# Making the last six of thirty x * v units of the second batch beside the first batch's third step

## The chip, the cores and the metric

The kernel runs on one core of one Trainium2 chip. Its engines are TensorE (PE in the profile; PEld is its weight load), VectorE (DVE), ScalarE (ACT), GpSimd (POOL) and SyncE (SP), which here issues every DMA. Each engine takes its instructions in the order in which the program issues them; an instruction that waits for a semaphore holds what stands behind it on its engine. Time is the device time of one launch in microseconds; the time before is 3616.57 us, the median of three runs (3615.18 to 3619.43).

## The reference

Two blocks follow each other. The first is a long convolution per channel, with a filter that a small network makes from position embeddings; the second is a layer with a cosine gate.

```python
# x, v: (4, 12480, 128); pos_emb: (12480, 64)
h = np.maximum(pos_emb @ w1, 0) @ w2 * np.exp(-0.01 * pos)[:, None]
u = x * v
y = causal_convolution(u, h)          # by FFTs of twice the length, along the sequence
x2 = (x * y).reshape(49920, 128)
g = x2 @ w_in                         # (49920, 2048)
out = (g * np.cos(g)) @ w_out         # (49920, 128)
```

## The kernel before

**Convolution.** The sequence of 12480 is laid out as 104 rows of 120, and the transform is done in two factors, 96 and 120. For each of the four batches there are these steps, all of them matmuls with tables, with evictions between them:

- the product u = x * v, in 30 units (`u_units`, lines 607 to 623): unit j takes two columns from below the middle and two from above, and needs one load of x and one of v (208 KB each, `u_load`, L429), two products (`u_multiply`, L440; for later batches one half on GpSimd, one on VectorE), and a sum and a difference (`u_sums`, L450; for later batches both on GpSimd), which are written into `slots`, the large buffer that holds a batch
- first step (`f1_units`, L634): forward along one factor; it needs all 30 units of u
- second step (`f2_units`, L645, and for the first batch `f2_both_units`, L665): forward along the other factor and the product with the filter's transform
- third step (`i1_units`, L697): inverse along one factor, 64 units. A unit is four matmuls of 120 columns into one PSUM bank (there are eight here), a copy by ScalarE (L534) and two sums by VectorE (L536), or, for every eighth unit, a copy by ScalarE (L527) and two sums by GpSimd (L530)
- fourth step (`i2_units`, L732): inverse along the other factor, in 30 groups, times x, stored to `zd`. Since group g's columns are free in `slots` as soon as it is done, the next batch's u is made beside this step (`later_u_units`, L625, in `inverse_units`, L757)

**MLP.** The rows of `zd` are loaded, turned, and go through up and down matmuls in 391 tiles of 16 steps. A step is an up matmul into one of three `ph` banks (`moe_up`), two passes over it on ScalarE (L819, L825) and two on VectorE (L820, L826), three sums on GpSimd for each pair of steps (L834, L837, L838), and the down matmuls into `acca` or `accb` (L851).

**Order.** The program writes the order out by hand. A convolution step is a generator that yields a price in units of MLP steps; the main loop (lines 1083 to 1115) resumes the generator `conv` after each MLP step while it owes prices (`convolve`). The function `units` (L575) is the common frame: for unit j it first calls `before(j + ahead)` (loads), then runs `parts` parts, in each of which it resumes the previous unit's `after` by one, and at the end yields `REST`, three MLP steps, so that what comes next finds the last results.

For the first batch, lines 768 to 773 resume the next batch's u maker in three of four parts of the fourth step, 85 times from its tenth part on, and run what is left of it afterwards; the fourth step's own last yield is worth seven MLP steps. Of the 92 times that the maker can be resumed, seven are left then: six parts of 2/3 step and REST, 7.0 MLP steps in all. Then the second batch's first step begins.

The third step of the first batch (lines 1028 to 1034) runs before the MLP has begun. Beside its 130 parts the generator `other = some_groups(pool)` is resumed at parts 14, 17, 21, 24 and so on. It makes six of the fourth step's tables ahead (`make_group`, L708): four pieces each, of which each is two scalings by ScalarE (into `some`, L329, and into `spare`, L334) and a sum by GpSimd (L335), and stores them to `td` (L717). `some` and `spare` have two buffers each. Between the third and the fourth group it makes four differences of `w_out` on GpSimd (L727), and at its end (part 112) it begins the fourth step: a load of x and a first table, made whole.

All DMAs stand in one queue, SP's, in the order of issue; a load into a buffer waits there until the last reader of the buffer's earlier content is done.

Of the kernel before, what the change touches and what calls it, by code (L numbers as in the profile page):

```python
# [10 lines left out]
F32 = mybir.dt.float32  # L11
# [3 lines left out]
ALU = mybir.AluOpType  # L15
# [19 lines left out]
def kernel(  # L35
# [46 lines left out]
    nc = tc.nc  # L82

    B, S, D = x.shape
# [3 lines left out]
    R = S // N2  # L88
    M = N1 * N2
    TURN = 4 * M  # L90
    H = N2 // 2
    ODD = 64
# [7 lines left out]
    CB = D // 2  # L100
# [5 lines left out]
    UA = 2  # L106
# [5 lines left out]
    ALONE = 8  # L112
    XV = 36
    LATER = 96
    AT = NFC // 2 + 2
    WCOL = 256

    dram = ctx.enter_context(tc.tile_pool(name="dram", bufs=1, space=DRAM))
# [3 lines left out]
    td = dram.tile([N2 // G, N1, G, 2, R], F32, name="td")  # L122
    wind = dram.tile([D, DFF], F32, name="wind")
    woutd = dram.tile([P, NFC // 2, 4 * CB], F32, name="woutd")
    csd = dram.tile([N2, 2, N2], F32, name="csd")
    rowsd = dram.tile([N1, 4, R], F32, name="rowsd")
    twd = dram.tile([N1, 2, N2], F32, name="twd")
# [7 lines left out]
    def mm(dst, left, right, start=True, stop=True):  # L135
        n = dst.shape[0]
        for lo, hi in ((0, CB), (CB, n)) if tiled[0] else ((0, n),):
            nc.tensor.matmul(dst[lo:hi], left[:, lo:hi], right, start=start, stop=stop)  # L138
# [272 lines left out]
    def load_pairs(t, src, b, first, second):  # L411

        start = src[b, first:first + UA, :]
        if len(t.shape) == 3:
            nc.sync.dma_start(t, bass.AP(
                tensor=start.tensor, offset=start.offset,
                ap=[[N2 * D, R], [(second - first) * D, 2], [1, UA * D]]))
            return
        for h, n2 in enumerate((first, second)):
            start = src[b, n2:n2 + UA, :]  # L420
            nc.sync.dma_start(t[:, h], bass.AP(tensor=start.tensor, offset=start.offset,
                                               ap=[[N2 * D, R], [D, UA], [1, D]]))


    def clear_gap(u):

        nc.gpsimd.memset(u[:, :, H:ODD, :], 0.0)

    def u_load(place, b, a):  # L429
        tiles = []  # L430
        for i, src in enumerate((x, v)):
            tiles.append(place(a // UA, i))
            load_pairs(tiles[i], src, b, H - UA - a, H + a)
        return tiles

    def u_multiply(tiles, half, engine):
        xt, vt = (t[:, half] for t in tiles)
        if len(vt.shape) > len(xt.shape):
            xt = xt.rearrange("p (n d) -> p n d", n=UA)
        engine.tensor_tensor(xt, xt, vt, op=ALU.mult)  # L440

    def u_sums(u, tiles, a, takers):
        both = tiles[0]
        if len(both.shape) == 4:
            both = both.rearrange("p h n (b i) -> p h n b i", i=2)
        else:
            both = both.rearrange("p h (n b i) -> p h n b i", n=UA, i=2)
        below, above = both[:, 0, ::-1, :, :], both[:, 1, :, :, :]
        for place, op, e in ((a, ALU.add, takers[0]), (ODD + a, ALU.subtract, takers[1])):
            e.tensor_tensor(u[0:R, :, place:place + UA, :].transpose([0, 2, 1, 3]),  # L450
                            below, above, op=op)
# [120 lines left out]

    def units(n, steps, before, mm, after, parts, ahead=2, skip=0):  # L575


        for j in range(min(ahead, n)):
            for _ in before(j) or ():
                pass  # L580
        yield 0.0
        last = iter(())
        for j in range(n):
            early = iter(before(j + ahead) or () if j + ahead < n else ())
            now = None
            for i in range(parts):
                if i == skip or 2 * (i - skip) == max(parts, 2):
                    now = mm(j, now, int(i > skip))
                if i == 0 and parts == 1:
                    now = mm(j, now, 1)  # L590
                next(last, None)
                next(early, None)
                yield steps / parts
            for _ in early:
                pass
            next(last, None)
            last = after(j, now)
        for _ in last:
            pass
        yield REST  # L600

    SOME = range(2, NG, 5)
    REST = 3.0
    U_STEPS, F1_STEPS, F2_STEPS, I1_STEPS, I2_STEPS = 2.0, 1.0, 3.4, 0.8, 1.5
    FIRST_STEPS, I2U_STEPS = 3.5, 3.4

    def u_units(b, u, engine, place, ahead, takers):

        tiles = {}

        def before(j):
            tiles[j] = u_load(place, b, j * UA)

        def after(j, _):
            for half in range(2):
                u_multiply(tiles[j], half, engine(j, half))
                yield
            if j == H // UA - 2:
                clear_gap(u)
            u_sums(u, tiles.pop(j), j * UA, takers(j))  # L620
            yield

        return units(H // UA, U_STEPS, before, lambda j, ps, i: None, after, 3, ahead=ahead)

    def later_u_units(b, u, engine, side):  # L625

        with tc.tile_pool(name="xv", bufs=3, side=side) as pool:
            def place(j, i):
                t = pool.tile([R, 2, UA * D], F32, name="xv"[i] + "t", bufs=3 - i)
                return t[:, :, :]  # L630

            yield from u_units(b, u, engine, place, 1, lambda j: (nc.gpsimd, nc.gpsimd))

    def f1_units(bank, u, share, evict=f1_evict):  # L634
        def mm(j, ps, i):
# [83 lines left out]
    def some_groups(pool):  # L719
        for g in SOME:  # L720
            t = pool.tile([N1, G, 2, R], F32, name="some", bufs=2)
            yield from make_group(pool, g, t, G)
            if g == SOME[2]:
                for dst, first_, second_, op in ((4, 1, 3, ALU.add), (5, 4, 0, ALU.subtract),
                                                 (1, 0, 1, ALU.subtract),
                                                 (6, 2, 5, ALU.subtract)):
                    nc.gpsimd.tensor_tensor(w_out_sb[:, :, dst, :], w_out_sb[:, :, first_, :],  # L727
                                            w_out_sb[:, :, second_, :], op=op)
                    yield
        next(backs[0])  # L730
# [26 lines left out]
    def inverse_units(bank, b):  # L757

        if b + 1 == B:
            yield from i2_units(bank, b, 3)
            return
        new = later_u_units(b + 1, slots[0:R, :, :, :],
                            lambda j, half: nc.vector if half else nc.gpsimd,
                            "right" if b else "left")
        parts = 4 if b == 0 else 2
        for i, steps in enumerate(i2_units(bank, b, 2)):
            if i > 2 * parts:
                for _ in range(i % parts > 0 if b == 0 else 1 + i % 2):  # L770
                    next(new, None)
            yield steps * (FIRST_STEPS if b == 0 else I2U_STEPS) / I2_STEPS
        yield from new
# [129 lines left out]
    with tc.manual_schedule():  # L903
        with tc.tile_pool(name="psum", bufs=8, space=PSUM) as psum, \
# [8 lines left out]
            parts = slots[:, :, 0:2 * N1, :].rearrange("p b (r k) i -> p r k b i", r=2)  # L913
# [87 lines left out]
            with tc.tile_pool(name="convert", bufs=1) as pool:  # L1001
                convert = convert_units(pool)
                next(convert)
                for i, _ in f1:
                    if i >= LATER and i % 9 in (0, 4):
                        if next(convert, True):
# [12 lines left out]
            for kept, here in ((rowsd, rows), (twd, tw_t)):  # L1019
# [6 lines left out]
            nc.sync.dma_start(w_out_sb[:, :, 0:4, :].rearrange("p c q d -> p c (q d)"),  # L1026
                              woutd[:, :, :])
            with tc.tile_pool(name="ready", bufs=1) as pool:
                other = some_groups(pool)
                for i, _ in enumerate(i1_units(bank, lambda b: b % 8 == 3)):  # L1030
                    if i > 10 and i % 7 in (0, 3):
                        next(other, None)
                for _ in other:
                    pass

# [31 lines left out]
        def load(n):  # L1067
            while made[0] * R < first_row(n + 1):
                next(conv)
            moe_load(mpool, n)  # L1070
# [4 lines left out]
        steps = [(n, c) for n in range(NALL) for c in range(NFC)]  # L1075
        hidden, pairs, gates, ots, turned, obs = {}, {}, {}, {}, {}, {}
        def convolve():
            nonlocal owed
            owed += 1.0
            while owed > 0.0:  # L1080
                owed -= next(conv, owed)

        for i in range(len(steps) + LAG):
# [5 lines left out]
            if i < len(steps):  # L1089
                n, c = steps[i]  # L1090
                if n == 0 and c == NFC // 2:
                    load(1)
                if c == (NFC - 2 if n else NFC - 1) and n + 2 < NALL:
                    load(n + 2)
                if c == AT and n > 0:
                    convolve()
                if c == AT and n - 1 in ots:
                    turned[n - 1] = moe_back(n - 1, ots.pop(n - 1))
                if c == (AT if n else NFC - 2) and n + 1 < NALL:
                    moe_turn(mpool, n + 1)  # L1100
# [10 lines left out]
            if i < len(steps):  # L1111
                if c == AT + 2 and n - 1 in obs:
                    moe_store(n - 1, obs.pop(n - 1))
            if i >= len(steps) or c != AT or n == 0:
                convolve()
# [30 lines left out]
```

## Time and profile before

| | |
|---|---|
| median of three runs | 3616.57 us (3615.18 to 3619.43) |
| the profiled execution | 3621.64 us |
| its span, first to last instruction | 3619.9 us |
| mean granted TensorE clock | 0.999 |
| TensorE busy | 3570.2 us (99%) |
| VectorE busy | 2833.8 us (78%) |
| GpSimd busy | 2749.9 us (76%) |
| ScalarE busy | 2230.3 us (62%) |
| first batch's third step, matmuls | 222.99 to 277.38 us |
| first batch's fourth step, first matmul | 278.90 us |
| second batch's first step, first matmul | 531.87 us |

Busy times are sums over one execution. A line of a group or of the order in time gives, after the line number, the operation, what it writes and from what it reads, and in brackets how long the engine had been idle before and what ended that. A line of a stretch gives the stretch, its length, and for each engine its busy time and number of instructions, then the granted clock, the DMA engines' share and GB/s.

### The profile page before, as it was taken

The page shows a single profiled execution, that of the slowest core. Times are in us where ns is not written, and L with a number is a line of the kernel's source. Part 1 is how long each engine was busy: PE and PEld are TensorE (multiplying, and loading weights), DVE is VectorE, ACT ScalarE, POOL GpSimd, SP SyncE. Part 2 cuts the span into 40 slices and gives each one's busy share as a digit, 9 for nine tenths or more (in the row PEclk, how much of TensorE's full clock was granted, in tenths as well). Part 3 has the DMA queues.
Part 4 walks back from the last instruction along what each step waited for, and adds up shares of the span by engine and source line. Part 5 has one row for each costly group of instructions (what it writes and reads, how often), then busy time and mean ns, then how long its engine had stood idle before and what let it go on. Part 6 is the DMA issues. An engine that isn't in the chain of part 4 may idle for free.

```text
span 3619.9 us, 102267 instructions
## 1 busy us (share of the span) xinstructions
PE 3570.2 (99%) x40826; PEld 2533.5 (70%) x40826; DVE 2833.8 (78%) x5289; ACT 2230.3 (62%) x4482; POOL 2749.9 (76%) x3237
## 2 busy tenths in 40 slices
PE   8999999999999999999999999999999999999999
PEld 7996767666677767666677776766667776666666
DVE  7888885688887885688887786688887667877877
ACT  7666766656654556665655556665655446666666
POOL 7777995688865885698864887588885458878877
PEclk9999999999999999999999999999999999999999
DMA  7545530122214640122202561022220350000000
GB/s 189 157 144 167 162 114 15 35 72 71 70 35 128 172 132 16 28 74 72 75 26 65 168 172 51 13 65 72 70 65 14 109 156 19 19 25 19 19 22 17
DMA packets 224195, 281.85 MB, mean 78 GB/s; under 512 B 23386, under 2 KB 161122, under 8 KB 223594
## 3 DMA queue, kind: packets, MB, share of 16 engines
q1 hardware_dynamic: 223722, 275.30, 26.4%
q8 instruction: 326, 5.34, 0.6%
q14 instruction: 147, 1.20, 0.1%
HBM read 194.75 MB, written 80.46 MB: 76 GB/s over the span
## 4 chain that ended last, share of the span: by engine, by line
PE 85%; DVE 4%; POOL 1%; ACT 1%; issue 1%; DMA 0%; SPq 0%; ACTq 0%; POOLq 0%; DVEq 0%
PE ph L138 31%; PE accb L851 17%; PE cv L138 17%; PE acca L851 13%; PE cv L458 3%; PE ph L142 1%; DVE gt L826 1%; DVE gt L820 1%; PE cv L142 1%; ACT gt L819 1%; DMA tm<-td 0%; POOL ts L834 0%; DVE xt L440 0%; DVE t L513 0%; POOL slots L450 0%
## 5 line engine op out<-in xcount | busy, mean ns | idle before, releaser
L820 DVE SCALAR_TENSOR_TENSOR gt<-ph,gt 128x512 f32<-128x512 f32 (+1 forms) x1380 | 948.0, 687 | 684.5 <-ACT gt L819 679.2
L819 ACT ACTIVATE gt<-ph 128x512 int32<-128x512 f32 (+1 forms) x1380 | 822.8, 596 | 1060.7 <-PE ph L138 1007.7
L834 POOL TENSOR_TENSOR ts<-gt 128x512 f32<-128x512 f32 (+2 forms) x784 | 1000.5, 1276 | 574.5 <-PE accb L851 570.3
L138 PE MATMUL ph<-at,w_in_sb 128*64 128x512 f32 (+1 forms) x5520 | 1428.5, 593 | 7.9 <-DVE gt L826 6.4
L825 ACT ACTIVATE gt<-gt 128x512 f32<-128x512 f32 (+1 forms) x1568 | 972.2, 620 | 6.4 <-DVE gt L820 5.2
L826 DVE TENSOR_TENSOR gt<-ph,gt 128x512 f32<-128x512 f32 (+1 forms) x1380 | 935.0, 678 | 0.0
L851 PE MATMUL accb<-ts,w_out_sb 128*64 128x128 f32 (+2 forms) x9408 | 649.1, 272 | 0.0
L837 POOL TENSOR_TENSOR ts<-ts,gt 128x256 f32<-128x256 f32 (+2 forms) x784 | 575.5, 734 | 61.5
L838 POOL TENSOR_TENSOR ts<-gt,ts 128x256 f32<-128x256 f32 (+2 forms) x784 | 575.5, 734 | 61.5
L851 PEld LDWEIGHTS acca<-gt,w_out_sb 128*64 128x64 f32 x6272 | 395.6, 136 | 263.2 <-issue 228.4
L851 PEld LDWEIGHTS accb<-ts,w_out_sb 128*64 128x64 f32 x9408 | 542.8, 137 | 0.0
L851 PE MATMUL acca<-gt,w_out_sb 128*64 128x128 f32 (+2 forms) x6272 | 478.1, 272 | 0.0
L851 PEld LDWEIGHTS accb<-gt,w_out_sb 128*64 128x64 f32 x3136 | 221.2, 136 | 251.8 <-issue 198.4
L138 PEld LDWEIGHTS ph<-at,w_in_sb 128*64 128x64 f32 x5520 | 345.4, 137 | 37.4 <-issue 17.7
L514 POOL TENSOR_TENSOR slots<-slots,t 120x256 f32<-120x256 f32 x383 | 278.0, 733 | 96.2 <-DVE t L513 62.5
L851 PE MATMUL accb<-gt,w_out_sb 128*64 128x128 f32 (+1 forms) x3136 | 310.0, 273 | 4.9 <-DVE ot L872 3.4
L138 PEld LDWEIGHTS cv<-slots,tm 96*40 96x40 f32 (+1 forms) x3840 | 226.3, 125 | 122.6 <-issue 113.1
L851 PE MATMUL acca<-ts,w_out_sb 128*64 128x128 f32 (+1 forms) x3136 | 307.3, 272 | 1.5 <-POOL ts L837 1.4
L138 PE MATMUL cv<-slots,tm 96*40 96x128 f32 (+1 forms) x3840 | 253.3, 273 | 5.5 <-DVE slots L536 3.4
L138 PEld LDWEIGHTS cv<-even,slots 120*64 120x64 f32 (+1 forms) x3072 | 165.6, 125 | 65.5 <-issue 60.4
L851 PEld LDWEIGHTS acca<-ts,w_out_sb 128*64 128x64 f32 x3136 | 200.2, 137 | 2.5 <-POOL ts L837 2.3
L458 PEld LDWEIGHTS cv<-c,slots 104*64 104x64 f32 (+1 forms) x1536 | 113.3, 137 | 112.1 <-issue 71.5
(136 smaller groups left out, 3845.2 us busy)
## 6 DMA issues: line engine op xcount, KB each, us to landing
h<-hd SPq DMA_DIRECT2D x144, 240.0 KB
tm<-td SPq DMA_DIRECT2D x96, 312.0 KB
xt<-in_x_dram SPq DMA_DIRECT2D x120, 208.0 KB
xs<-in_x_dram SPq DMA_DIRECT2D x120, 208.0 KB
zd<-xs SPq DMA_DIRECT2D x119, 208.0 KB
tile<-zd SPq DMA_DIRECT2D x96, 256.0 KB
vt<-in_v_dram SPq DMA_DIRECT2D x90, 208.0 KB
w<-wd SPq DMA_DIRECT2D x144, 105.0 KB
```

Of the source, the lines that this page charges most:

```text
L138: nc.tensor.matmul(dst[lo:hi], left[:, lo:hi], right, start=start, stop=stop)
L142: nc.tensor.transpose(dst, src, ident[0:n, 0:n])
L458: nc.tensor.matmul(dst[lo:hi], u[:, b, lo:hi, i], c1[0:u.shape[0], r:r + 2, :].rearrange("p r k -> p (r k)"), start=True, stop=True)
L514: (engine if r else nc.gpsimd).tensor_tensor(y[:, r], y[:, r], t[:, r], op=op)
L819: nc.scalar.activation(turns, ph[:, 0:m], AF.Identity, bias=phase)
L820: nc.vector.scalar_tensor_tensor(out=part, in0=ph[:, 0:m], scalar=phase, in1=turns, op0=ALU.add, op1=ALU.subtract)
L825: nc.scalar.activation(part, part, AF.Sin, scale=scale)
L826: nc.vector.tensor_tensor(part, ph, part, op=ALU.mult)
L834: nc.gpsimd.tensor_tensor(ts[:, 0:2, 0:half], gt[:, :, half:2 * half], gt[:, 0, 0:2 * half].rearrange("p (h n) -> p h n", h=2), op=ALU.sub ...
L837: nc.gpsimd.tensor_tensor(t[2], t[1], b11, op=ALU.add)
L838: nc.gpsimd.tensor_tensor(t[3], b21, t[2], op=ALU.subtract)
L851: nc.tensor.matmul(acc[h * CB:(h + 1) * CB, place, 0:r], w_out_sb[:, pair, weight, :], right[:, h * r:(h + 1) * r], start=(pair == 0 and i ...
```

## The change

In the second batch, the last six of the 30 units of u are no longer made beside the first batch's fourth step. They are made beside its third step (`early_u_units`): their x and v are loaded into buffers of their own (two each) in the pool `ready`, one half is multiplied by GpSimd and one by VectorE, GpSimd takes the sum and the difference into a tile `kept` (two buffers), and the tile is stored to a new DRAM buffer `ud`. The generator is resumed at every sixth part of the third step: the first loads are issued at parts 5 and 11, those of units 2 to 5 at parts 29, 47, 65 and 83; the sums of unit 0 to 4 at 41, 59, 77, 95 and 113, and all of unit 5's arithmetic at 119.

Beside the fourth step, the maker runs 24 units as before and then six of `kept_u_units`: each loads one tile from `ud` (into the buffers of `xt`, three) and ScalarE copies its two halves into `slots`. A part of these is priced at 0.2 MLP steps, and the 24 units end without REST. The maker can now be resumed 94 times, so 9 are left after the fourth step's end, 4.6 MLP steps in all. Other batches are as before.

```diff
@@
+    EARLY = 6
+    ud = dram.tile([EARLY, R, 2, CB, 2 * UA], F32, name="ud")
@@
-    def units(n, steps, before, mm, after, parts, ahead=2, skip=0):
+    def units(n, steps, before, mm, after, parts, ahead=2, skip=0, rest=3.0):
...
-        yield REST
+        yield rest
@@
-    def u_units(b, u, engine, place, ahead, takers):
+    def u_units(b, u, engine, place, ahead, takers, count=H // UA):
...
-        return units(H // UA, U_STEPS, before, lambda j, ps, i: None, after, 3, ahead=ahead)
+        return units(count, U_STEPS, before, lambda j, ps, i: None, after, 3, ahead=ahead,
+                     rest=REST if count == H // UA else 0.0)
+
+    def early_u_units(b, pool):
+        tiles = {}
+        def place(j, i):
+            t = pool.tile([R, 2, UA * D], F32, name="xv"[i] + "s", bufs=2)
+            return t[:, :, :]
+        def before(j):
+            tiles[j] = u_load(place, b, H - (EARLY - j) * UA)
+        def after(j, _):
+            for half in range(2):
+                u_multiply(tiles[j], half, nc.vector if half else nc.gpsimd)
+                yield
+            both = tiles.pop(j)[0].rearrange("p h (n b i) -> p h n b i", n=UA, i=2)
+            kept = pool.tile([R, 2, CB, 2 * UA], F32, name="kept", bufs=2)
+            for q, op in ((0, ALU.add), (1, ALU.subtract)):
+                nc.gpsimd.tensor_tensor(
+                    kept[:, q].rearrange("p b (n i) -> p n b i", i=2),
+                    both[:, 0, ::-1, :, :], both[:, 1, :, :, :], op=op)
+            nc.sync.dma_start(ud[j, :, :, :, :], kept[:, :, :, :])
+            yield
+        return units(EARLY, 0.0, before, lambda j, ps, i: None, after, 3, ahead=1)
+
+    def kept_u_units(u, pool):
+        kept = {}
+        def before(j):
+            kept[j] = pool.tile([R, 2, CB, 2 * UA], F32, name="xt", bufs=3)
+            nc.sync.dma_start(kept[j][:, :, :, :], ud[j, :, :, :, :])
+        def after(j, _):
+            a = H - (EARLY - j) * UA
+            for q, place in enumerate((a, ODD + a)):
+                nc.scalar.copy(
+                    out=u[0:R, :, place:place + UA, :].rearrange("p b j i -> p b (j i)"),
+                    in_=kept[j][:, q])
+                yield
+            if j == EARLY - 2:
+                clear_gap(u)
+            yield
+        return units(EARLY, 0.6, before, lambda j, ps, i: None, after, 3, ahead=2)
+
-    def later_u_units(b, u, engine, side):
+    def later_u_units(b, u, engine, side, partly=False):
+        count = H // UA - (EARLY if partly else 0)
...
-            yield from u_units(b, u, engine, place, 1, lambda j: (nc.gpsimd, nc.gpsimd))
+            yield from u_units(b, u, engine, place, 1, lambda j: (nc.gpsimd, nc.gpsimd), count)
+            if partly:
+                yield from kept_u_units(u, pool)
@@ inverse_units
-                            "right" if b else "left")
+                            "right" if b else "left", b == 0)
@@ the third step of the first batch
+                ahead = early_u_units(1, pool)
                 other = some_groups(pool)
                 for i, _ in enumerate(i1_units(bank, lambda b: b % 8 == 3)):
                     if i > 10 and i % 7 in (0, 3):
                         next(other, None)
+                    if i % 6 == 5:
+                        next(ahead, None)
+                for _ in ahead:
+                    pass
                 for _ in other:
                     pass
```

## The prediction

> **What bounds the kernel now.** I read the first two parts of the page, then tables of busy time by stretch around the two places that the change touches, then the order in time on each engine there, and the waits of TensorE.
>
> ```profile
> PE 3570.2 (99%) x40826; PEld 2533.5 (70%) x40826; DVE 2833.8 (78%) x5289; ACT 2230.3 (62%) x4482; POOL 2749.9 (76%) x3237
> ```
>
> TensorE is busy for 3570.2 of 3619.9 us. It has the same matmuls after the change, so only its idle time and its clock can move the span: 50 us in all, and only what lies at the two places counts.
>
> First place, the third step of the first batch, 223 to 279 us (columns: stretch, its length, busy time of PE, PEld, DVE, ACT, POOL, clock, DMA share, GB/s):
>
> ```profile
> 262.00:266.00 4.00, 4.00 (x41) 4.00 (x41) 3.09 (x9) 3.52 (x12) 3.04 (x6) 1.00 0.15 39
> 270.00:274.00 4.00, 4.00 (x41) 4.00 (x40) 1.76 (x6) 3.80 (x12) 3.86 (x7) 1.00 0.31 87
> 274.00:278.00 4.00, 3.37 (x33) 3.17 (x31) 4.00 (x13) 2.49 (x7) 1.36 (x3) 1.00 0.65 184
> ```
>
> TensorE is the bound up to 277.4 us, ScalarE has about 0.3 us of every 4 free, and the last 5 us are VectorE's. In order of time on four engines:
>
> ```profile
> 222.99 54.39 PE L138 MATMUL ps<-even,slots 120*96 120x120 f32 x512 [1.92 <-POOL slots L514]
> 259.01 0.30 SPq L717 DMA_DIRECT2D td<-some  x1
> 264.59 0.47 ACT L329 ACTIVATE some<-rows,tw_t 96x208 f32<-96x208 f32 x1
> 273.59 5.17 DVE L536 TENSOR_TENSOR slots<-ps,other 96x240 f32<-96x240 f32 x16 [2.14 <-ACT other L534]
> 278.90 3.11 PE L138 MATMUL cv<-slots,tm 96*64 96x128 f32 x48 [1.52 <-DVE slots L536]
> ```
>
> The 512 matmuls run without a gap, 0.85 us for each of 64 units; the fourth inverse step starts at 278.90, released by VectorE, which had got 2.14 us behind because ScalarE made four tables in one go (270.33 to 273.2).
>
> Second place, the end of the first batch's fourth step, where the remaining x * v is made and the second batch's first step waits for it:
>
> ```profile
> 525.00:530.00 5.00, 4.27 (x40) 2.24 (x36) 4.58 (x8) 3.16 (x6) 4.84 (x7) 1.00 0.16 58
> 530.00:535.00 5.00, 2.99 (x24) 2.25 (x26) 1.30 (x3) 0.68 (x2) 4.76 (x7) 0.87 0.16 45
> 535.00:540.00 5.00, 5.00 (x51) 4.40 (x50) 1.94 (x4) 2.77 (x6) 3.04 (x4) 0.79 0.35 101
> ```
>
> ```profile
> 507.36 0.33 SPq L415 DMA_DIRECT2D xt<-in_x_dram  x1
> 521.87 0.31 SPq L415 DMA_DIRECT2D vt<-in_v_dram  x1
> 522.27 1.11 SPq L897 DMA_DIRECT2D out_dram<-tile  x3
> 531.09 1.41 POOL L450 TENSOR_TENSOR slots<-xt 104x256 f32<-104x256 f32 x2
> 531.87 1.06 PE L458 MATMUL cv<-c,slots 104*64 104x192 f32 x3 [2.35 <-POOL slots L450]
> ```
>
> GpSimd is full to 532.5 us, TensorE waits 2.35 us for its last sums, and the clock then falls to 0.87 and 0.79. The SP lines show one thing more: the load of vt stood on SP's queue from 507.7 to 521.87 waiting for its buffer, and the stores behind it left only after it.
>
> **The change, part by part.**
>
> *Work taken from the fourth step.* A unit costs GpSimd one product and two sums, 3 x 0.73 = 2.2 us, VectorE one product (median 0.95 us there) and SP two loads. Six units are 13.2 us of GpSimd and 5.7 us of VectorE. But they are the last six, made from about 484 us on (the products' rows). Before that nothing changes, so the gain is what TensorE loses from there: idle 0.73 + 2.01 us in 525 to 535, and a clock short by 0.13 and 0.21 over 5 us each, 1.70 us. Sum 4.4 us. At the most the 0.82 us idle in 480 to 490 and 0.27 in 510 to 520 go too: 5.5 us.
>
> *The clock.* The fall behind a 2.35 us wait is in the rows. [...] I take the row.
>
> *Work put in its place.* Twelve ScalarE copies of 104x256. No such row exists; the nearest are 0.345 us (96x240) and 0.59 us (128x512), so 0.36 us each, 4.3 us. Five run in the fourth step, where ScalarE is 60 to 75% busy: nothing, while that cover lasts (4.3 us at worst). The rest bunch: the program resumes the maker 85 times inside the fourth step; before, 7 of 92 resumptions were left, after, 9 of 94, and these carry seven copies within some two up/down steps of the MLP, 2.5 us, after a pause of 7 steps. Such a step takes 1.5 to 1.6 us and ScalarE has about 0.4 us of it free, so some 1.6 us is late, and the three ph banks take part of that. I take 1.0 us (0 to 2.5: all hidden, all paid). Kept gain 4.4 - 1.0 = 3.4 us. The steps left before the first step shrink from 7.0 to 4.6; that moves the convolution 2.4 steps ahead and takes no work away: 0.
>
> *GpSimd in the third step.* The sums, products and their neighbours run in order. Putting the 18 added operations (13.2 us) in their places among the old ones, with old ready times, GpSimd runs 1 to 2.5 us late between 248 and 266 us. ScalarE's spare has two buffers, written some 2.9 us ahead, so this alone costs under 0.5 us: covered by eight PSUM banks. VectorE's six products: 0.41 to 0.95 us each, and only the sixth falls into VectorE's closing run: 0.7 us on the path.
>
> *SP's queue in the third step.* This is the step that I think decides. The loads of unit j+2 reuse the buffers of unit j (two each), so they wait on SP until GpSimd's sums of unit j are done, and everything behind waits along. Loads are issued at iterations 29, 47, 65, 83 of the loop, the sums that free them at 41, 59, 77, 95. The stores of the made tables are issued at 28, 42, 56, 84, 98, 112. The fourth, at 84, stands directly behind the load of the sixth unit. It left at 259.01; now it can leave only after the fourth sums, which in the placing above end at 266.7: load x, load v, then the store at 267.6 (0.4 us an issue). The first such store, at 235.95, moved its data from 236.75 to 238.1. With 416 KB of loads ahead at some 250 GB/s (1.6 us) the fourth has landed at about 270.5. The group begun at iteration 98 uses the same buffer ("some" has two), and ScalarE wants to write it at 264.59. ScalarE is therefore held 5.9 us, and behind it in its queue stand the copies that empty TensorE's banks: TensorE fills eight banks in 8 x 0.85 us and then waits about 2.3 us at 270.6. ScalarE then needs 8.2 us to the end of its table burst, where it took 8.6, and VectorE's closing run follows with 0.7 us more: the fourth step starts 5.9 - 0.4 + 0.7 = 6.2 us late. Bounds: 0.4 us (the store finds its way free; one product of 0.41 us; nothing is removed here, so no gain) and 8.5 us (GpSimd 2.3 us later still). The other five stores have 1.3 us or more to spare.
>
> *The clock there.* TensorE ends its 64 units near 281 and waits for VectorE until 285: 1.2 us between 0 and the 1.7 us measured at 530.
>
> *Loads and stores.* Twelve loads and six stores of 208 KB move into a step with a DMA share of 0.31; six loads replace twelve at 0.5 to 0.6. Beyond the queue's order: 0.
>
> Sum: +6.2 + 1.2 - 3.4 = **+4.0 us**. The profiled execution took 3621.64 us (span 3619.9), which makes 3625.6; it lies 5.07 us above the median of 3616.57, so for the median 3620.6 us.
>
> **Rivals.**
>
> *The third step hides it.* The store is not held long enough to stop ScalarE. For it: eight banks, a GpSimd 60% busy, 6 us of slack between the old store and the write. Against it: the order on SP above. Only 0.7 us is paid: 3616.6 + 0.7 - 3.4 = 3613.9 us.
>
> *Slower: the sixth stored unit lands late.* Its load waits for a buffer that ScalarE's copies of the third stored unit free, only about one MLP step before ScalarE itself wants it, and a load needs some 2.5 us from issue (0.8 us until data moves, 0.85 us for 208 KB, the rest to be noticed). ScalarE then stands in front of the MLP's sines; where TensorE waits over 2 us the clock falls as at 530, and the whole 3.4 us is gone: 3616.6 + 7.4 = 3624.0 us, just slower. Against it: ScalarE has 2.6 us of other work in between.
>
> *Faster.* All of 5.5 us and no cost gives 3611.1 us, which is still within 0.2%; faster needs a gain that no row here shows.
>
> **How the numbers follow.** 0.2% is 7.2 us, about what a measurement of this kernel can tell from no change. My forecast 0.55 (3620.6 us; its own ends 3615 and 3626), the hiding third step 0.22, the late unit 0.17, faster beyond the rows 0.04, another cause of slower 0.02. Within 0.2% comes out at 0.9 of the first, nearly all of the second, none of the third: 0.71. Slower 0.17 + 0.02 + 0.05 = 0.24; faster 0.05. The range goes from 3612.5 (the second case with 1.4 us to spare) to 3626.5 (the third with 2.5 us).
>
> **What would show it.** The fourth store of a made table leaves at about 267.6 instead of 259.0; ScalarE stands idle for some 6 us before a table write near 265; TensorE waits about 2 us near 270.6; the fourth step starts near 285 instead of 278.9; the wait of 2.35 us for L450's sums and the low clock behind it are gone. I am wrong if ScalarE never waits for that store, or if the second batch's first step waits again, for ScalarE's copies.

## The result, and the profile after

The changed kernel takes 3626.18 us (median of 14 executions, 3623.0 to 3627.81) against 3618.05 us before (14, 3615.18 to 3622.68): ratio 1.002 with a 95% interval of 1.0013 to 1.0028, 8.1 us slower. That is at the edge of the 0.2% that the prediction called the limit of a measurement; the interval does not reach 1, and in microseconds it goes from 4.7 to 10.1. The forecast was 4.0 us slower, a little less than its lower end.

Busy time on the first part of the profile's page after:

```profile
PE 3571.6 (99%) x40826; PEld 2534.1 (70%) x40826; DVE 2829.5 (78%) x5289; ACT 2232.7 (62%) x4494; POOL 2751.3 (76%) x3237
```

The instructions are what the diff says (12 more on ScalarE), and the sums of busy time have hardly moved: what changed is waits. The order in time of the changed kernel around the third step (line numbers have moved: L331 is the first table scaling, L417 the loads, L770 the store of a made table, L538 and L532 the third step's last sums):

```profile
222.75 46.25 PE L140 MATMUL ps<-even,slots 120*96 120x120 f32 x448 [1.93 <-POOL slots L516]
265.49 0.31 SPq L417 DMA_DIRECT2D xs<-in_x_dram  x1
266.30 0.39 SPq L770 DMA_DIRECT2D td<-some  x1
270.63 0.47 ACT L331 ACTIVATE some<-rows,tw_t 96x208 f32<-96x208 f32 x1 [7.63 <-DMA td<-some]
272.60 8.44 PE L140 MATMUL ps<-even,slots 120*96 120x120 f32 x64 [3.60 <-DVE slots L538]
284.82 5.35 PE L140 MATMUL cv<-slots,tm 96*64 96x128 f32 x48 [3.78 <-POOL slots L532]
```

(A matmul of the program stands here as two instructions, so the 256 matmuls of the third step count as 512.) The loads of the sixth early unit leave at 265.49, when the fourth sums have freed their buffers, and the fourth table store 0.8 us behind them, 7.3 us later than before (259.01). ScalarE stands idle for 7.63 us until that store has landed, TensorE runs out of banks after 448 of its 512 matmuls and waits 3.60 us, and the fourth step starts at 284.82 instead of 278.90. Its first 48 matmuls then take 5.35 us where they took 3.11.

The stretches after, same columns as before:

```profile
266.00:270.00 4.00, 3.00 (x30) 2.80 (x28) 0.00 (x0) 0.00 (x0) 0.00 (x0) 1.00 0.78 235
270.00:274.00 4.00, 1.40 (x11) 1.43 (x12) 1.98 (x6) 3.37 (x10) 1.86 (x3) 0.92 0.23 85
274.00:278.00 4.00, 4.00 (x27) 4.00 (x27) 2.32 (x7) 3.78 (x13) 3.89 (x7) 0.65 0.08 23
278.00:282.00 4.00, 3.04 (x30) 2.84 (x28) 2.93 (x9) 2.72 (x9) 3.43 (x7) 1.00 0.71 207
282.00:286.00 4.00, 1.18 (x12) 1.21 (x14) 2.68 (x9) 2.30 (x7) 2.69 (x4) 0.70 0.50 140
286.00:290.00 4.00, 4.00 (x40) 3.78 (x36) 1.84 (x4) 1.11 (x4) 0.62 (x1) 0.50 0.38 103
290.00:294.00 4.00, 3.36 (x18) 2.01 (x18) 0.00 (x0) 1.02 (x2) 0.00 (x0) 0.50 0.81 228
294.00:298.00 4.00, 4.00 (x30) 2.35 (x29) 1.54 (x3) 1.50 (x4) 0.00 (x0) 0.59 0.18 55
```

```profile
525.00:530.00 5.00, 4.78 (x50) 3.30 (x48) 2.88 (x5) 3.90 (x8) 2.75 (x4) 1.00 0.31 90
530.00:535.00 5.00, 4.79 (x54) 3.07 (x51) 3.56 (x6) 4.49 (x12) 4.49 (x5) 1.00 0.34 91
535.00:540.00 5.00, 5.00 (x57) 3.71 (x57) 3.42 (x6) 3.23 (x7) 3.65 (x5) 1.00 0.38 120
```

In 266 to 270 ScalarE, VectorE and GpSimd do nothing at all. The clock falls twice: behind the wait of 3.60 us, to 0.92 and 0.65 up to 278 us, and behind that of 3.78 us, to between 0.50 and 0.70 from 282 to 298. The first fall costs little: from ScalarE's held table write to the start of the fourth step it is 14.2 us here and 14.3 us before. In 525 to 540, where the kernel before lost 2.7 us idle and 1.7 us of clock, TensorE is now idle for 0.43 us and the clock is full: the wait that the change was to take away is gone.

Following the MLP's first pass on ScalarE (1380 of them in both traces, the n-th start against the n-th) shows where the time goes. "Late" is against the one profiled execution of before:

| MLP pass | 0 | 16 | 64 | 110 | 120 | 300 | 1379 |
|---|---|---|---|---|---|---|---|
| starts before, us | 284.5 | 314.5 | 424.3 | 524.4 | 550.3 | 929.8 | 3607.7 |
| the change is late by | 8.9 | 10.4 | 10.4 | 10.2 | 6.5 | 5.2 | 4.7 |

So 5.9 us at the start of the fourth step, 10.4 us once the MLP runs, and 3.7 us given back at the second batch's first step. The two profiled executions differ by 4.8 us (3626.46 and 3621.64), the medians by 8.1: the profiled execution of before lies 3.6 us above its median. A part of that has a place: in the profiled execution of before the clock fell at the beginning of the third step, in that of the change it did not, after the same wait of 1.9 us. First before, then the change:

```profile
222.00:226.00 4.00, 3.01 (x15) 3.01 (x16) 1.80 (x5) 0.35 (x1) 1.43 (x4) 0.63 0.56 164
```

```profile
222.00:226.00 4.00, 3.25 (x31) 3.22 (x32) 2.38 (x7) 1.07 (x3) 1.20 (x4) 1.00 0.46 142
```

The 512 matmuls take 54.4 us with this fall and 52.8 us without it (experiments below): 1.6 us by chance. Against a before without this fall the lateness would be about 7.5 us at the start of the fourth step, 12.0 us once the MLP runs, 8.1 us at pass 120 and 6.3 us at the end. The rest of the gap between profiles and medians has no place in these traces.

### The profile page after: what moved, and what is told of

The parts are those of the page before. It is cut to its first block, busy times and chain, and to the rows that moved or that the text cites. A ratio compares the mean times of both kernels' runs of the same rounds, so it can differ in the third digit from the quotient of the medians.

```text
span 3624.7 us, 102378 instructions
## 1 busy us (share of the span) xinstructions
PE 3571.6 (99%) x40826; PEld 2534.1 (70%) x40826; DVE 2829.5 (78%) x5289; ACT 2232.7 (62%) x4494; POOL 2751.3 (76%) x3237
## 4 chain that ended last, share of the span: by engine, by line
PE 90%; DVE 5%; POOL 2%; ACT 1%; issue 1%; DMA 1%; SPq 0%; ACTq 0%; DVEq 0%; POOLq 0%
PE ph L140 31%; PE accb L904 17%; PE cv L140 17%; PE acca L904 13%; PE cv L460 3%; PE ps L460 2%; PE ps L140 1%; PE ph L144 1%; DVE gt L879 1%; DVE gt L873 1%; PE cv L144 1%; PE ps L400 1%; ACT gt L872 1%; PE ps L496 1%; PE ps L493 0%
## 5 line engine op out<-in xcount | busy, mean ns | idle before, releaser
L140 PE MATMUL cv<-at,w_in_sb 128*64 128x512 f32 (+1 forms) x752 | 191.7, 586 | 0.0
```

## The experiments

My theory: the time is lost because one table store stands behind loads in SP's queue (the hold), and then because TensorE, left waiting, starts the fourth step at half clock; the gain at the second batch's first step is real and small. Rivals: GpSimd, which has 13.2 us more to do in the third step, or the added transfers, cost the time; the second loss is the order of the start, not the clock; GpSimd's relief is worth more than the one wait.

All medians, each with its own runs of the kernel before on the same chip:

| run | median, us | before, us | ratio and 95% interval | late at pass 16 / 120 / 1379, us |
|---|---|---|---|---|
| the change | 3626.18 | 3618.05 | 1.002, 1.0013 to 1.0028 | 10.4 / 6.5 / 4.7 |
| e1, three load buffers | 3617.85 | 3619.23 | 0.9996, 0.9987 to 1.0005 | 5.4 / 1.6 / -0.1 |
| e2, two parts later | 3619.62 | 3619.23 | 1.0, 0.9991 to 1.0009 | 3.1 / -1.0 / -2.1 |
| e3, early half alone | 3630.53 | 3619.23 | 1.0032, 1.002 to 1.0043 | 9.8 / 9.5 / 8.5 |
| e4, late half alone | 3616.00 | 3619.23 | 0.9992, 0.9983 to 1.0001 | 0.6 / -3.5 / -3.4 |
| e5, matmuls in the wait | 3623.72 | 3618.81 | 1.0013, 1.0004 to 1.0021 | 5.2 / 1.4 / -0.1 |
| e6, three buffers of some | 3617.07 | 3618.81 | 0.9997, 0.9989 to 1.0006 | 4.7 / 0.6 / -1.5 |
| e7, four units | 3619.31 | 3618.81 | 1.0002, 0.9993 to 1.0011 | -0.2 / -3.3 / -4.5 |
| e8, e1 with matmuls | 3616.37 | 3618.81 | 0.9995, 0.9987 to 1.0004 | -0.8 / -4.8 / -6.6 |
| e9, both waits filled | 3616.04 | 3618.70 | 0.9994, 0.9985 to 1.0002 | -0.7 / -4.5 / -4.6 |
| e10, before, both filled | 3620.15 | 3618.70 | 1.0005, 0.9997 to 1.0014 | -1.4 / -1.9 / -1.5 |
| e11, four units, filled | 3616.79 | 3618.70 | 0.9996, 0.9987 to 1.0005 | 0.4 / -2.6 / -3.7 |

The last column is of one profiled execution each, against the one of before, whose 3621.64 us lie 2.4 to 3.6 us above all the medians of before in this table. It tells where in the kernel time is lost or won; how much, the medians tell. Executions of one kernel lie 2 to 10 us apart.

### The hold: e1, e2, e6

```diff
-            t = pool.tile([R, 2, UA * D], F32, name="xv"[i] + "s", bufs=2)
+            t = pool.tile([R, 2, UA * D], F32, name="xv"[i] + "s", bufs=3)
```

> The loads of the early units get three buffers each instead of two; work and order stay the same. Queue theory: the load of the sixth unit then waits for the sums of the third (part 77), not of the fourth (95), so the fourth table store leaves near 259 to 260 us, ScalarE does not wait for it, TensorE runs its 512 matmuls without a gap, the fourth step starts 0.5 to 1.5 us later than before instead of 5.9, the clock stays at 1.00 there, and the kernel ends 2 to 3.5 us before the kernel before, near 3615. Rival, GpSimd is full: it still has 13.2 us more to do, the stretches 242 to 262 stay at 4.00 of 4.00, the fourth step still starts 4 to 6 us late, and the time stays near 3626.

```diff
-                    if i % 6 == 5:
+                    if i % 6 == 1 and i > 1:
                         next(ahead, None)
```

> The early units are resumed at parts 7, 13, 19 and so on instead of 5, 11, 17; two buffers as in the change, the same instructions. The load of the sixth unit is then issued at part 85, behind the fourth table store (84) instead of ahead of it. Queue theory: the store leaves near 259 to 260 us, no hold, the fourth step starts within 1.5 us of 278.9, the time is near 3615. Rival, GpSimd is full or the added transfers are too many: nothing of that changes, the time stays near 3626.

```diff
-            t = pool.tile([N1, G, 2, R], F32, name="some", bufs=2)
+            t = pool.tile([N1, G, 2, R], F32, name="some", bufs=3)
```

> The changed kernel with three buffers of 'some' instead of two. The fourth table store still leaves late, near 266 us, behind the load of the sixth unit, but nothing has to wait for it. If the hold is the buffer's, ScalarE does not stand still, the fourth step starts about 1.3 us later than before by its distance from the first of the 512 matmuls (55.9 us before, 62.1 in the change, 57.2 with three load buffers), and the time is near that with three load buffers, 3617 to 3618. If SP's queue hurts in another way (the loads behind it), it stays at 61 to 62 us and 3626.

Each leaves all the work and all the transfers in place, and each takes back what the change costs: +8.1 us become -1.4, +0.4 and -1.7, none of which can be told from no difference. Stretches, the store and the start of the fourth step with three load buffers (e1):

```profile
254.00:258.00 4.00, 4.00 (x41) 4.00 (x40) 2.92 (x9) 3.57 (x12) 4.00 (x5) 1.00 0.56 162
258.00:262.00 4.00, 4.00 (x41) 4.00 (x40) 3.52 (x11) 3.32 (x12) 4.00 (x8) 1.00 0.03 6
...
282.00:286.00 4.00, 4.00 (x38) 3.50 (x32) 1.78 (x4) 1.21 (x4) 0.63 (x1) 0.51 0.42 106
```

```profile
223.71 54.46 PE L140 MATMUL ps<-even,slots 120*96 120x120 f32 x512 [2.02 <-POOL slots L516]
262.67 0.41 SPq L770 DMA_DIRECT2D td<-some  x1
280.92 4.35 PE L140 MATMUL cv<-slots,tm 96*64 96x128 f32 x48 [2.75 <-POOL slots L532]
```

GpSimd is as full as the rival wants it (4.00 of 4.00 from 254 to 262), and still TensorE runs its 512 matmuls without a gap. ScalarE's wait for the store falls from 7.63 to 1.1 us in e1 and 1.6 us in e2, and there is none in e6. The fourth step starts 57.2, 57.6 and 56.8 us after the first of the 512 matmuls, against 55.9 before and 62.1 in the change. In e6 the store still leaves late, and it does no harm:

```profile
268.89 0.39 SPq L770 DMA_DIRECT2D td<-some  x1
...
280.46 4.01 PE L140 MATMUL cv<-slots,tm 96*64 96x128 f32 x48 [2.33 <-POOL slots L532]
```

So the late start was for the most part neither GpSimd's load nor the transfers: it was one store behind one pair of loads, together with a table that had two buffers. The 3615 us expected of e1 and e2 were too good by 3 to 5 us, though (e6's 3617 to 3618 held). What is left in e1 is GpSimd's tail, 1.3 us at the start (the fourth step is released by its sums, L532), and behind the wait of 2.75 us a clock of 0.51: the second loss does not need the long hold.

### The two halves: e3, e4

```diff
-                            "right" if b else "left", b == 0)
+                            "right" if b else "left")
```

> Only the first half of the change: the six units are made and stored beside the third step, but not used; all thirty are made again beside the fourth. It is the cost by itself. Queue theory with the low clock: fourth step 5.9 us late, 4.4 us more in its first 20 us, then nothing given back: 10.4 us over before, 3628 us. Rival, the cost is only the shift of the start: 6 us, 3624.

```diff
-                ahead = early_u_units(1, pool)
...
-            nc.sync.dma_start(kept[j][:, :, :, :], ud[j, :, :, :, :])
+            a = H - (EARLY - j) * UA
+            load_pairs(kept[j].rearrange("p h b n -> p h (b n)"), x, 1, H - UA - a, H + a)
```

> Only the second half: nothing is made early; the last six units are loaded straight from x (without the product with v and without sums, so that part of the second batch is left out) and copied in by ScalarE. It is the gain by itself. My theory: the wait of 2.35 us for the last sums and the low clock behind it go, ScalarE's copies cost about 0.5 us, 3.7 us under before, 3614.4 us. Rival, GpSimd bounds the whole fourth step and 13 us less of its work counts in full: 8 us or more under before, 3610.

The early half alone costs 11.3 us, the late half alone saves 3.2 us; the sum, 8.1 us, is what the change costs. That it fits to the tenth is luck: the intervals of the two halves are over 6 us wide, and that of e4 just reaches no difference. In e3 the lateness stays at 9.5 us through pass 300, so nothing later gives it back; in e4 it is 0.2 to 0.6 us up to pass 110 and -3.5 us at pass 120, so the gain sits at the second batch's first step and nowhere else. 13.2 us less for GpSimd in the fourth step is worth 3 to 4 us: the rival of 8 us or more lies outside e4's interval, which ends 6.2 us under before.

### The clock: e5, e8

```diff
                 for _ in other:
                     pass
+                idle = bank()
+                for _ in range(16):
+                    nc.tensor.matmul(idle[0:N2, 0:N2], cs[:, 0, :], cs[:, 1, :],
+                                     start=True, stop=True)
```

> The changed kernel with 16 more matmuls of 120x120 (tables by tables, into a PSUM bank that nobody reads) behind the 512 of the third step, 16 x 0.21 = 3.4 us, so that TensorE is busy while it waits 3.8 us for the last sums. Nothing else moves. Clock theory: the clock stays at 1.00 to 302 us, the first 48 matmuls of the fourth step take 3.1 us instead of 5.35, the first MLP steps are 6 us late instead of 10.4, the time is 4.4 us under that of the change, near 3621.8. Rival, the second 4.4 us come from the order of the start (tables, loads held on SP): 3626 as in the change.

e8 is e1 with 11 of these.

> Six units, three load buffers, and 11 matmuls (2.3 us) in the wait of 2.75 us that is left at the end of the third step. Clock theory: the clock stays at 1.00, the first MLP steps are 1.3 to 2 us late instead of 4.7 (less the 0.7 us by which that run began later), and the time is 2 to 3 us under the kernel with three buffers alone, 2 to 4 us under the kernel before. Otherwise as with three buffers alone.

In e5, with 16 matmuls in the wait (32 instructions) and the rest of the program as in the change:

```profile
280.19 3.52 PE L1095 MATMUL ps<-even 120*120 120x120 f32 x32
284.20 3.09 PE L140 MATMUL cv<-slots,tm 96*64 96x128 f32 x48 [0.48 <-POOL slots L532]
```

The fourth step starts 61.4 us after the first of the 512 matmuls, nearly as late as in the change (62.1), but its first 48 matmuls take 3.09 us again, the clock reads 1.00 from 258 to 298, and at pass 16 the kernel is 5.2 us late instead of 10.4. So the second half of the lateness was the clock: in this execution the same order of the start adds nothing to the 5.3 us with which the MLP begins. The median gives back only 2.5 us of the expected 4.4, and the executions form two groups: five from 3620.1 to 3622.1 us, the profiled one (3621.99) among them, and six from 3623.7 to 3627.0. Why the six keep the loss is open. The clock can also fall in the earlier wait: it did in the change and in e3 (0.92 and 0.65, 0.86 and 0.72 from 270 to 278 us), and not in e5's profile. It may be that in the six it did, and that the 16 matmuls then ran slower and held the start themselves; no profile here shows it.

e8 does most of what was expected of it: no stretch under 1.00 from 258 to 298, 3.09 us for the first 48 matmuls, its 512 matmuls in 52.80 us, and a median 2.4 us under its runs of before, where e1 was 1.4 us under its own. That is 1 us between them and not the 2 to 3 expected, but the executions lie between 3615.1 and 3618.8, those of e1 between 3614.8 and 3621.7. Its first MLP steps are 0.8 us early, not 1.3 to 2 us late, because in this execution the clock did not fall at 222 us, where e8 fills nothing.

What the waits did to the clock, from the profiles of all the kernels:

| kernel | wait before the fourth step, us | clock just after | first 48 matmuls, us |
|---|---|---|---|
| before, e4 | 1.52 | 1.00 | 3.11, 3.08 |
| e6 | 2.33 | 0.50 | 4.01 |
| e1 | 2.75 | 0.51 | 4.35 |
| e7 | 3.04 | 1.00 | 3.06 |
| e2 | 3.17 | 0.63 | 4.52 |
| e3 | 3.77 | 0.50 | 5.35 |
| the change | 3.78 | 0.50 | 5.35 |
| e9, e10, e8, e5, e11 (filled) | 0.26 to 0.75 | 1.00 | 2.98 to 3.13 |

Of the six unfilled waits of over 2 us five had a fall behind them, of the five filled ones none. How long the clock stayed low differed too; in e2 it was full again from 286 us:

```profile
282.00:286.00 4.00, 4.00 (x42) 3.67 (x38) 1.84 (x4) 1.30 (x4) 0.62 (x1) 0.63 0.49 132
286.00:290.00 4.00, 3.36 (x35) 2.06 (x36) 0.78 (x2) 1.75 (x4) 0.00 (x0) 1.00 0.89 248
```

### A better version: e7, e9, e10, e11

e7 is e1 with four early units (`EARLY = 4`).

> Four early units instead of six, three load buffers. With three buffers alone the six units still make GpSimd end its part of the third step late (TensorE waits 2.75 us for L532, and the clock falls to 0.5 for 8 us, 3.2 us lost). Four units end at part 83 and take 4.4 us less from GpSimd. Expected: fourth step 0 to 0.5 us late, clock 1.00 there, the wait of the second batch's first step still gone, 3.2 us under the kernel before, as the second half alone. If the last units of the fourth step need all six to be made early, 0 to 1 us under.

Its profile is as expected, its median is not: 0.5 us over before, where 3.2 us under was forecast.

```profile
222.91 52.80 PE L140 MATMUL ps<-even,slots 120*96 120x120 f32 x512 [1.92 <-POOL slots L516]
...
278.76 3.06 PE L140 MATMUL cv<-slots,tm 96*64 96x128 f32 x48 [3.04 <-DVE slots L538]
```

The profiled execution (3617.16 us, against a median of 3619.31) passed both waits with a full clock; the others need not have.

e9 is e8 with 10 more matmuls (from `c1`, 104x96) in the wait of 1.9 us ahead of the third step; e10 is the kernel before with these 10 and 6 at the end of the third step; e11 is e9 with four units.

> Six early units, three load buffers, 11 idle matmuls at the end of the third step as in the run before, and 10 more (1.6 us) in the wait of 1.9 us at its beginning, where the clock falls in half of the executions profiled so far and costs 1.6 us. Clock theory: no stretch under 1.00 from 222 to 300 us, the 512 matmuls in 52.8 us every time, the times closer together and 3 us or more under the kernel before, near 3615.5. If the falls at 222 us have another cause than the wait, the time stays near 3616.4 with the spread of before.

> The kernel before, without the change, with the same 10 idle matmuls at the beginning of the third step and 6 (1.3 us) in the wait of 1.5 us at its end. It tells what the filling is worth by itself. Clock theory: 0.8 us under the kernel before in the median (1.6 us in half of the executions), so 3618. What e9 has beyond that is the change's.

> Four early units, three load buffers, both waits filled. Its profile without the filling had the fourth step at 278.8 and ended 4.5 us under before, while its median did not move. If that median was made by executions in which the clock fell in one of the two waits, it is now 4 us under before, 3614.5, with a narrow spread; if six units are needed, it is 1 to 2 us slower than e9.

e9 has the lowest median after e4, which leaves work out: 2.7 us under before. Its 11 executions lie between 3614.9 and 3617.2, before's 27 between 3616.3 and 3620.9; the interval of the ratio still reaches 1.0002, so faster is likely and not proven. With e10, which ran beside it, the comparison is clearer: the two differ by the change with three load buffers (and 11 matmuls in place of 6), e9 is 4.1 us faster, and its slowest execution (3617.21 us) is faster than e10's fastest (3617.78). e11 is 1.9 us under before, 0.75 us behind e9: four units do not beat six, and the 4 us were not there. e10 misses what was expected: its profile has the third step at full clock (52.80 us for the 512 matmuls) and is 1.4 us early at pass 64, yet its median is 1.4 us over before, which cannot be told from no difference. The profile does not show where the early start goes: it keeps 1.9 us at pass 120 and 1.5 us at the end, against a profiled execution of before that was slower than any of the 27 runs of before beside e10 (3616.34 to 3620.93 us). What it does show is that the second batch's first step still loses what it lost before, 2.6 us idle and 1.7 us of clock:

```profile
525.00:530.00 5.00, 2.84 (x25) 1.24 (x20) 4.40 (x8) 2.75 (x5) 4.76 (x8) 1.00 0.23 57
530.00:535.00 5.00, 4.54 (x35) 3.90 (x37) 0.05 (x1) 0.33 (x1) 4.84 (x6) 0.66 0.45 111
```

Filling the waits alone has therefore shown no gain, and by the comparison with e10 what e9 has over before comes with the change.

## Why the prediction was right or wrong

- **SP's queue, "the step that I think decides": right.** The fourth store left at 266.30 (267.6 foretold), ScalarE wrote its table at 270.63 (270.5), the fourth step began at 284.82 (285), 62.1 us behind the first of the 512 matmuls, 6.2 us more than before (6.2 foretold). The mechanism was right; that the numbers meet so closely is partly luck. The store left 1.3 us early and took 4.3 us to let ScalarE write instead of 2.9. The 6.2 us are against a profile of before in which the clock had fallen at 222 us; against e10, where it had not (54.3 us), they are 7.7. And the fourth step was released by GpSimd's last sums (L532), not by VectorE's closing run as foretold. ScalarE's and TensorE's waits were longer than said, 7.63 and 3.60 us against 5.9 and 2.3, since in this execution the clock did not fall at 222 us and both came to the wait earlier. e1, e2 and e6 remove the hold in three ways.
- **The clock at the start of the fourth step: the term that failed.** I put 1.2 us, between 0 and 1.7, the latter measured at 530 us. It was 4.4 us (10.4 less 5.9 late, before rounding), and e5 takes it back in its profile. At 530 the MLP and the convolution kept TensorE full (5.00 of 5.00 us from 535 to 540) and the clock, 0.87 and 0.79 in the two stretches, was 1.00 again from 540; at the start of the fourth step the work is a chain from engine to engine, and the clock stayed between 0.50 and 0.70 for 16 us. So the loss measured at one place was no upper bound at another. That the thinner work is the reason is argued and not shown: in e2, with as thin a start, the clock was at 1.00 again from 286 us. Taking this one term as measured turns +4.0 into +7.2 us.
- **The gain: right.** 3.4 us foretold (4.4 less 1.0 for ScalarE's copies); 3.7 us in the profile, 3.2 us alone in e4. The copies cost TensorE at most 0.43 us in 525 to 540. A copy of 104x256 took 0.39 us, or 0.33 us each in a row of four; I had put 0.36.
- **Work hidden in the third step: right as far as it was tested.** GpSimd ran late without stopping TensorE; VectorE's closing products took 0.41 and 0.56 us. But GpSimd's tail costs 1.3 us of start in e1, where I had charged 0.7 us to VectorE.
- **The rivals.** "The third step hides it" is out by the 7.63 us. "The sixth stored unit lands late" did not happen: ScalarE made its four and two copies from 530.08 and 532.31 without a wait. Slower by 0.2% came true, at a chance of 0.24, but by the clock at the fourth step and not by that mechanism. I gave 0.71 to a time within 0.2%; the measured 8.1 us are 0.22%. The 3626.18 us lie in the stated range by only 0.3 us, and its upper end was made for that late unit, while the main case was to end at 3626: that the range holds is luck. Of the 5.6 us between 3620.6 and 3626.18 the starting point makes 1.5, the median of 14 being 3618.05 where three had given 3616.57.
- **The clock behind a wait.** That I counted the 1.7 us of low clock at 530 with the wait was right: with the wait gone, TensorE's clock is 1.00 from 525 to 540. The length of a wait did not tell by itself whether the clock fell: the table above has falls behind waits of 2.33, 2.75 and 3.17 us and none behind 3.04, and at 222 us a wait of 1.9 to 2.0 us had a fall in five of the ten kernels profiled without a filling there. So the "over 2 us" of the late unit's rival is no limit that a run shows.

## What to carry to other kernels

Work that is moved beside a full stage brings its loads along, and a load that waits for its buffer holds the stores behind it in the same queue (here the fourth table store left at 266.30 us instead of 259.01, and ScalarE stood idle for 7.63 us): write down, for each queue, what stands directly behind a waiting load and who needs it, and give the loads one more buffer or issue them after the store. Price a wait of the matmul engine together with the low clock that may follow it (here it followed waits of 1.9 to 3.8 us, not every one), and do not take a loss measured elsewhere for its upper bound: it was 1.6 us at 222, 1.7 us at 530 and 4.4 us at the start of the fourth step. Undo a change by halves: here the halves, +11.3 and -3.2 us, add up to the whole, and say that the idea was worth about 3 us and its place in the queue cost more.

## What the runs showed of the hardware that I had not expected

The clock of TensorE fell behind waits of 1.91 to 2.02 us at 222 us in five profiles and did not behind waits of 1.91 to 2.03 us in five others, of kernels that are alike up to there; where it fell, the 512 matmuls took 54.39 to 54.47 us, where it did not and nothing else held them, 52.80 us. Filling the waits did not make the times meet in general: the executions lie 2.3 us apart in e9, but 4.0 in e11 and 6.3 in e10, which are filled too. Behind a fall at the start of the fourth step the clock stayed under 1.00 for very different times: 16 us in the change (282 to 298), in e6 up to 294 us, in e1 still 0.71 from 290 to 294 us, in e2 up to 286 us. With a wait filled by matmuls whose result nobody reads the clock was 1.00 behind it in every profile (at the fourth step in e5, e8, e9, e10 and e11, at 222 us in e9, e10 and e11), and by itself the filling did not make the kernel before faster (e10: 3620.15 us against 3618.70).
